# Another written order for the same instructions: block-sparse attention, Fourier mixing and an MLP on one core

## The chip, the core and the metric

The kernel runs on one core of one Trainium2 chip. The core has a matrix engine (TensorE, "PE" in the profile; "PEld" is its weight load), a vector engine (VectorE, "DVE"), a scalar engine (ScalarE, "ACT"), a general engine (GpSimd, "POOL") and an engine that here only issues DMAs (SyncE, "SP"). Each engine works through its own instructions in order; between engines only semaphores order the work. The metric is the device time of one execution in microseconds, the median of several runs.

## The reference

Four batches, eight heads, 768 positions, head size 64. Shortened:

```python
k_rep = k.reshape(B, H, 12, 64, D).mean(axis=3)              # one mean key per block of 64
gate  = einsum('bhsd,bhnd->bhsn', q, k_rep)                  # where(causal by block, gate, -1e9)
sel   = top-3 blocks of gate, and the position's own block
scores = where(sel and causal, q @ k.T / 8, -1e9)
x  = softmax(scores) @ v                                     # heads side by side: (4, 768, 512)
u  = x + real(fft(fft(x, axis=1), axis=2))
un = (u - mean(u)) / sqrt(var(u) + 1e-6)                     # over the last axis
out = u + relu(un @ w_ch1) @ w_ch2                           # 512 -> 2048 -> 512
```

## The kernel before

The work is cut into small steps, each a function that issues a handful of instructions on one or two engines. A step is named by a token with its indices. A long string, `ORDER` (lines 112 to 179), lists 1011 tokens, and one loop at the end of the builder issues them:

```python
with tc.manual_schedule(engines={ET.SP, ET.PE, ET.DVE, ET.Activation, ET.Pool}):
    consts_first()
    for x in ORDER.split():
        n, a = x.split(":")
        WORK[n](*[int(i) for i in a.split(",")])
```

So the order on every engine is the order of the string: no planner moves anything. How tokens of different engines stand to each other in the string has no effect by itself, except where two steps use the same buffer: then the one written first goes first.

**Attention.** The 32 heads are worked in 16 pairs; pair P belongs to batch P // 4. The tokens of a pair, with their engine:

- `Lk`, `Lq`, `Lv` (SP): loads of K, Q and V rows in fp32. Buffers: three for K, three for Q, two for V, so a load waits until the pair before it in the buffer has been used.
- `tk`, `tq` (PE, L292): six transposes into one PSUM tile of 128 × 768. PSUM is a pool of four such buffers, shared by everything that PE produces.
- `ks` (DVE, L297) reduces the transposed K to block sums; `kc` (ACT, L308 or L311) copies the same PSUM tile to fp16. `kh` (DVE) halves the sums. `qc` (DVE, L316) copies Q out of PSUM, `qs` (POOL, L225) casts it.
- `g` (PE) gate products; `gt`, `gx`, `gl`, `gm` (DVE) transpose, take the top three, compare, and transpose back the block mask; `K` (POOL) and `iz`, `Lc`, `Li` put mask and indicator rows where the score product adds them.
- `s:P,i` (PE) scores of query block i; `e` (ACT, L431) the exponential; `d` (POOL, L437) the causal cut on the diagonal; `vc` (POOL) casts V; `v` (PE) product with V; `x` (DVE) division by the row sum.

**Mixing, per batch b.** `fs`, `fd`, `f` (DVE) fold rows into even and odd parts; `pg` (POOL) a guard. `y:b,h` (PE, L519 and L525) is the transform along the sequence. `ty` (ACT, L532) and `tr` (DVE, L538) both copy the tile of `y` out of PSUM, straight and reversed. `m:b,j` (PE, L552 and L553) is the transform along the features; `u` (DVE) adds x and sums, `xu` (ACT) subtracts the mean. `xt` and `un` transpose the result into `unT`: by PE and DVE for batch 0, by two DMA transposes on SP for each `un` of the other batches (L593). `bn`, `nv` (DVE) and `nr` (POOL) find the deviation, which is applied only at the end.

**MLP.** `w:b,i` (PE, L629 and L631) first product, `r` (relu out of PSUM: DVE for every fourth, L639, else ACT, L641), `c:b,j,h` (PE, L656 and L648) second product in two halves, `o:b,j` (DVE, L668) scale and add, `od:b,j` (SP, L673) store of 128 rows, 256 KB (128 KB for the last tile of batch 3, which is split by columns). `W` and `X` (POOL) load the two weight matrices and cast them from fp32 to fp16 on the way, in three and two pieces.

The work of the four batches is interleaved: while PE does the MLP of one batch, the attention of the next pairs and the mixing of the next batch run between its products. Up to the first `w:0` there is only attention and mixing; this text calls it the prologue.

Of the kernel before, what the change touches and what calls it, by code (L numbers as in the profile page):

```python
# [109 lines left out]


ORDER = """
Lk:1 Lq:1 Lk:2 Lq:2 tk:0 ks:0 tq:0 Lq:3 Lk:3 kh:0 qc:0 iz:1 tk:1 qs:0 kc:0 g:0 ks:1 iz:0 gt:0 tq:1
kc:1 gx:0 Lq:4 Lv:0 Lk:4 Lv:1 kh:1 gl:0,0 tk:2 gl:0,1 gm:0 kc:2 qc:1 s:0,3 s:0,2 ks:2 e:0,3 qs:1
tq:2 Lq:5 Lk:5 s:0,5 qc:2 g:1 e:0,5 e:0,2 kh:2 s:0,4 gt:1 qs:2 s:0,0 e:0,4 gx:1 s:0,1 d:0,2 tq:3
gl:1,0 e:0,0 gl:1,1 tk:3 gm:1 e:0,1 d:0,0 qc:3 g:2 d:0,3 kc:3 d:0,5 s:1,5 gt:2 d:0,4 s:1,0 e:1,5
qs:3 ks:3 s:1,4 e:1,0 tq:4 d:0,1 gx:2 vc:0 e:1,4 s:1,3 qc:4 s:1,1 Lv:2 e:1,3 s:1,2 gl:2,0 kh:3
tk:4 gl:2,1 e:1,2 d:1,3 gm:2 g:3 d:1,4 ks:4 d:1,0 v:0 d:1,5 gt:3 vc:1 kc:4 gx:3 e:1,1 s:2,5 Lv:3
Lq:6 LF:0 Lq:7 Lk:6 Lk:7 LT:0 s:2,3 kh:4 gl:3,0 e:2,5 gl:3,1 s:2,4 e:2,3 d:1,1 x:0 tq:5 qs:4 e:2,4
g:4 d:2,3 gm:3 qc:5 s:2,0 d:2,4 s:2,2 d:1,2 e:2,0 gt:4 d:2,5 tk:5 vc:2 gx:4 e:2,2 s:2,1 ks:5 d:2,0  # L120
Lv:4 Lq:8 Lk:8 s:3,1 e:2,1 v:1 gl:4,0 kh:5 gl:4,1 kc:5 d:2,1 gm:4 d:2,2 s:3,2 x:1 e:3,1 vc:3 g:5
e:3,2 Lv:5 Lc:0 d:3,1 s:3,5 gt:5 s:3,0 fs:0,1 e:3,5 s:3,3 d:3,2 gx:5 e:3,0 s:3,4 fs:1,1 tq:6
gl:5,0 e:3,3 fs:0,0 v:2 gl:5,1 fs:1,0 e:3,4 d:3,3 qc:6 d:3,0 s:4,5 x:2 d:3,4 s:4,4 e:4,5 d:3,5
s:4,0 qs:5 v:3 e:4,0 gm:5 fs:2,0 fs:2,1 e:4,4 s:5,5 x:3 s:4,1 e:5,5 s:5,1 e:4,1 fd:2,0 s:4,2 s:5,0
fs:3,1 e:5,1 fs:3,0 s:5,2 fd:2,1 e:5,0 fd:3,1 s:4,3 fd:3,0 e:5,2 tk:6 f:0,1 f:0,2 e:4,3 Lk:9 Lq:9
tk:7 f:0,3 e:4,2 f:0,0 y:0,1 ks:7 pg:0 W:0 kc:6 y:0,0 tr:0,1 d:4,0 kc:7 d:4,4 d:4,5 ks:6 d:5,5
d:4,1 ty:0,1 tr:0,0 s:5,3 d:5,2 s:5,4 d:4,3 kh:6 W:1 ty:0,0 m:0,2 qs:6 e:5,3 u:0,2 m:0,1 vc:4
e:5,4 m:0,0 u:0,1 xu:0,2 d:5,4 tk:8 d:5,1 d:4,2 u:0,0 xu:0,1 d:5,0 xt:0,2 W:2 g:6 un:0,2 xu:0,0
xt:0,1 gt:6 tq:8 un:0,1 kc:8 xt:0,0 qc:8 tq:7 un:0,0 qs:8 v:4 Lq:10 Lk:10 Lv:6 Lq:11 qc:7 bn:0,3
w:0,4 d:5,3 qs:7 bn:0,1 w:0,5 r:0,4 gx:6 ks:8 w:0,6 r:0,5 gl:6,0 kh:7 gl:6,1 x:4 w:0,7 r:0,6 gm:6  # L130
w:0,3 r:0,7 s:6,5 r:0,3 s:6,1 e:6,5 s:6,3 e:6,1 kh:8 s:6,2 fs:4,0 bn:0,4 w:0,2 e:6,2 d:6,1 X:0
e:6,3 g:7 w:0,0 d:6,5 gt:7 r:0,2 d:6,3 vc:6 gx:7 s:6,4 r:0,0 vc:5 s:6,0 e:6,4 tk:9 Li:0 gl:7,0
Lv:7 tq:9 gl:7,1 e:6,0 gm:7 w:0,11 Lq:12 Lv:8 K:7 qc:9 kc:9 g:8 r:0,11 v:5 gt:8 d:6,0 ks:9 w:0,8
qs:9 gx:8 w:0,10 x:5 r:0,8 d:6,4 d:6,2 gl:8,0 s:7,5 s:7,2 r:0,10 kh:9 fs:4,1 w:0,1 bn:0,5 e:7,5
vc:7 e:7,2 tq:10 gl:8,1 Lv:9 r:0,1 X:1 gm:8 s:7,4 qc:10 w:0,15 d:7,2 e:7,4 K:8 bn:0,0 g:9 r:0,15
s:7,0 w:0,9 gt:9 e:7,0 gx:9 vc:8 tq:11 r:0,9 d:7,0 Lv:10 s:7,1 qc:11 d:7,5 tk:10 d:7,4 e:7,1
gl:9,0 s:7,3 ks:10 v:6 e:7,3 kh:10 gl:9,1 kc:10 gm:9 d:7,3 s:8,4 bn:0,2 d:7,1 w:0,12 vc:9 x:6
e:8,4 K:9 Lv:11 Lk:11 Lq:13 Lq:14 Lk:12 Lk:13 v:7 r:0,12 g:10 x:7 s:8,3 w:0,13 e:8,3 gt:10 nv:0
s:9,4 r:0,13 fs:5,1 s:9,1 fs:7,0 vc:11 w:0,14 e:9,4 fs:6,1 e:9,1 fs:7,1 s:8,1 fs:6,0 fs:5,0
c:0,2,0 r:0,14 fd:7,1 fd:6,1 e:8,1 gx:10 s:9,0 fd:7,0 s:9,2 e:9,0 fd:6,0 s:8,2 gl:10,0 c:0,3,0  # L140
f:1,3 e:9,2 f:1,2 e:8,2 gl:10,1 f:1,0 s:8,0 gm:10 s:9,3 d:8,2 e:8,0 y:1,1 d:8,1 d:9,0 e:9,3 nr:0
c:0,0,0 tr:1,1 ty:1,1 s:9,5 c:0,2,1 e:9,5 d:8,0 d:9,3 tk:11 K:10 s:8,5 c:0,1,0 Lk:14 ks:11 kc:11
c:0,3,1 f:1,1 d:9,5 e:8,5 d:9,1 qs:10 tq:12 o:0,2 y:1,0 od:0,2 kh:11 d:8,4 o:0,3 pg:1 vc:10 qc:12
c:0,1,1 od:0,3 ty:1,0 d:9,4 Lv:12 Lv:13 qs:11 tr:1,0 g:11 c:0,0,1 gt:11 d:8,3 d:8,5 gx:11 qs:12
m:1,0 o:0,0 m:1,1 od:0,0 o:0,1 d:9,2 od:0,1 v:8 u:1,1 m:1,2 u:1,0 xu:1,1 c:0,4,0 gl:11,0 xu:1,0
un:1,1 x:8 s:10,3 gl:11,1 un:1,0 c:0,4,1 u:1,2 e:10,3 d:10,3 fs:8,0 s:10,5 s:10,2 bn:1,3 e:10,5
tk:12 e:10,2 fs:8,1 v:9 gm:11 Lk:15 Lq:15 ks:12 xu:1,2 K:11 bn:1,0 tq:13 kc:12 un:1,2 c:0,5,0
qc:13 vc:13 bn:1,4 s:11,2 d:10,5 x:9 s:11,4 vc:12 e:11,2 c:0,5,1 bn:1,1 Lv:14 Lv:15 e:11,4 s:11,0
o:0,5 s:11,5 w:1,11 e:11,5 od:0,5 o:0,4 e:11,0 kh:12 bn:1,5 od:0,4 s:11,3 w:1,7 e:11,3 r:1,11
s:10,1 d:11,3 r:1,7 d:11,0 s:10,0 e:10,1 d:11,4 g:12 d:10,2 tk:13 d:11,5 e:10,0 gt:12 d:11,2  # L150
s:11,1 ks:13 d:10,1 w:1,0 e:11,1 d:10,0 kh:13 fs:9,0 fs:9,1 s:10,4 r:1,0 d:11,1 gx:12 w:1,14
e:10,4 gl:12,0 gl:12,1 g:13 gm:12 r:1,14 d:10,4 w:1,12 K:12 gt:13 kc:13 gx:13 w:1,6 bn:1,2 r:1,12
tq:14 gl:13,0 r:1,6 qs:13 v:10 qc:14 gl:13,1 s:12,3 gm:13 s:12,5 v:11 x:10 e:12,3 K:13 e:12,5
s:12,0 x:11 w:1,8 e:12,0 fs:10,0 vc:15 s:12,1 r:1,8 s:12,2 fs:10,1 s:13,4 e:12,1 d:12,3 w:1,5
fs:11,1 d:12,5 e:13,4 fs:11,0 d:12,1 fd:10,0 w:1,10 r:1,5 fd:11,0 fd:10,1 s:13,0 fd:11,1 r:1,10
w:1,4 f:2,0 e:13,0 f:2,2 s:13,1 f:2,1 e:12,2 w:1,2 e:13,1 tk:14 r:1,4 w:1,3 ks:14 r:1,2 f:2,3
kc:14 s:12,4 kh:14 r:1,3 pg:2 y:2,0 d:13,4 vc:14 nv:1 e:12,4 qs:14 w:1,9 tr:2,0 w:1,13 ty:2,0
# [630 lines left out]
```

## Time and profile before

| | |
|---|---|
| time, median of 3 runs | 297.56 us (297.54 to 297.93) |
| span of the profiled execution | 295.6 us; 1.96 us of the median lie outside it |
| PE busy | 286.5 us (97%) |
| DVE, ACT, POOL busy | 192.5, 164.2, 111.1 us |
| TensorE clock granted | 1.00 throughout |
| DMA | 33.53 MB, mean 113 GB/s |
| row loads, us to landing | K 3.5, Q 3.9 (192 KB), V 4.7 (384 KB) |
| casting loads, us to landing | `W` 8.4 (768 KB), `X` 10.2 (1024 KB) |
| stores, DMA transposes, us to landing | 2.1, 2.5 |
| one copy `kc` of pairs 0 to 6, one reduce `ks` | 0.8, 0.94 us |

In lines of groups and of the timeline the order is: (start,) busy time or duration, engine, line of the kernel, operation, output <- inputs with their shapes, count, and in brackets the idle time before it with what ended it. In the windows each engine's busy time stands beside its number of instructions. In the waits, "A <- B: total, times, longest" is idle time of A that an instruction of B ended.

### The profile page before, as it was taken

How to read it: one execution, taken by the hardware profiler on the slowest of the kernel's cores; microseconds unless marked ns; L12 is line 12 of the kernel's file. 1: busy time of each engine (PE TensorE's matmuls, PEld its weight loads, DVE VectorE, ACT ScalarE, POOL GpSimd, SP SyncE). 2: the span in 40 equal slices, each digit the busy share in tenths (PEclk: the TensorE clock that was granted, in tenths of full speed). 3: DMA queues.
4: the chain of work that ended last, by engine and by line, in shares of the span. 5: the costliest groups of instructions: out<-in, count | busy, mean ns of one | idle time of the engine just before them, and what ended most of it. 6: DMA issues, size and time to landing. Idle time of an engine off the chain costs nothing.

```text
span 295.6 us, 6738 instructions
## 1 busy us (share of the span) xinstructions
PE 286.5 (97%) x2633; PEld 180.2 (61%) x2633; DVE 192.5 (65%) x597; ACT 164.2 (56%) x205; POOL 111.1 (38%) x286
## 2 busy tenths in 40 slices
PE   8899999999999999999999999999999999999995
PEld 4566767765676556656757667446666554555453
DVE  2999999986988638987796577714493282700132
ACT  3698989749578841677788843165524250155000
POOL 2267528528776289064753363220303000110000
PEclk9999999999999999999999999999999999999999
DMA  8999999997999727477000005311000052300023
GB/s 197 268 228 230 262 245 199 195 230 118 226 185 211 168 55 186 118 164 176 3 0 2 0 9 136 38 72 71 2 1 2 32 103 44 142 0 2 0 91 125
DMA packets 93200, 33.53 MB, mean 113 GB/s; under 512 B 85936, under 2 KB 89968, under 8 KB 93168
## 3 DMA queue, kind: packets, MB, share of 16 engines
q1 hardware_dynamic: 87504, 28.47, 40.6%
q0 software_dynamic: 3664, 4.19, 9.1%
q10 hardware_dynamic: 2000, 0.44, 0.7%
q8 instruction: 21, 0.34, 0.5%
q14 instruction: 11, 0.09, 0.1%
HBM read 28.63 MB, written 6.29 MB: 118 GB/s over the span
## 4 chain that ended last, share of the span: by engine, by line
PE 84%; DVE 7%; ACT 6%; DMA 1%; issue 1%; DVEq 0%; ACTq 0%
PE c L656 26%; PE h L629 19%; PE h L631 10%; PE sc L414 7%; PE av L449 6%; ACT pt L431 5%; PE tp L292 5%; PE yp L519 2%; PE mx L552 2%; DVE q L316 2%; PE mx L553 1%; PE warmps L693 1%; DVE u L566 1%; PE g L342 1%; PE c L648 1%; PE sc L409 1%
## 5 line engine op out<-in xcount | busy, mean ns | idle before, releaser
L431 ACT ACTIVATE pt<-sc 128x1024 f16<-128x1024 f32 (+1 forms) x96 | 83.3, 923 | 26.6 <-PE sc L414 19.7
L629 PE MATMUL h<-unT,w 128*128 128x512 f16 x256 | 85.1, 379 | 0.0
L656 PE MATMUL c<-w_sb,hT 128*128 128x512 f16 x368 | 83.8, 379 | 0.0
L631 PE MATMUL h<-unT,w 128*128 128x256 f16 x256 | 69.7, 272 | 0.4 <-DMA unT<-x 0.4
L641 ACT ACTIVATE hT<-h 128x768 f16<-128x768 f32 x48 | 37.8, 813 | 43.7 <-PE h L631 43.7
L656 PEld LDWEIGHTS <-hT 128*128 128x128 f16 x368 | 35.6, 98 | 39.3 <-issue 0.5
L437 POOL TENSOR_SCALAR_AFFINE_SELECT pt<-pt 128x256 f16<-128x256 f16 x96 | 37.5, 414 | 58.5 <-ACT pt L431 57.6
L629 PEld LDWEIGHTS <-w 128*128 128x128 f16 x256 | 25.0, 97 | 29.2 <-issue 1.3
L668 DVE SCALAR_TENSOR_TENSOR u<-c,rs,u 128x512 f32<-128x512 f32 (+1 forms) x25 | 17.5, 725 | 31.2 <-PE c L656 30.4
L639 DVE TENSOR_SCALAR hT<-h 128x768 f16<-128x768 f32 x16 | 15.3, 955 | 29.7 <-PE h L631 29.6
L578 ACT ACTIVATE x<-u,nm 128x512 f16<-128x512 f32 x24 | 15.9, 715 | 22.5 <-DVE nm L572 22.3
L292 PE MATMUL tp<-id,nat 128*128 128x128 f32 x192 | 27.5, 284 | 0.6 <-ACT pt L431 0.3
L631 PEld LDWEIGHTS <-w 128*128 128x128 f16 x256 | 25.0, 98 | 4.3
L225 POOL TENSOR_SCALAR_AFFINE_SELECT qk<-mt 32x160 f16<-32x160 f16 x72 | 23.1, 341 | 10.8 <-DVE mt L386 9.1
L414 PE MATMUL sc<-qk 96*128 96x512 f16 (+3 forms) x144 | 26.8, 305 | 0.0
L225 POOL TENSOR_SCALAR_AFFINE_SELECT qk<-q 64x768 f16<-64x768 f32 (+1 forms) x25 | 20.6, 825 | 14.8 <-DVE q L316 14.1
L292 PEld LDWEIGHTS tp<-id,nat 128*128 128x128 f32 x192 | 22.2, 146 | 5.7 <-issue 1.6
L449 PE MATMUL av<-v,pt 128*128 128x65 f16 x672 | 23.0, 193 | 0.1
L449 PEld LDWEIGHTS <-pt 128*128 128x128 f16 x672 | 22.0, 97 | 1.7 <-POOL pt L437 0.5
L297 DVE TENSOR_REDUCE kr<-tp 128x12 f32<-128x768 f32 x16 | 15.1, 945 | 5.9 <-PE tp L292 5.9
L222 POOL TENSOR_TENSOR t<-vr,rs 128x6 f32<-128x6 f32 x12 | 2.4, 199 | 43.5 <-DVE rs L609 42.9
L414 PEld LDWEIGHTS <-qk 96*128 96x128 f16 x144 | 13.3, 97 | 8.9 <-issue 0.5
(95 smaller groups left out, 351.2 us busy)
## 6 DMA issues: line engine op xcount, KB each, us to landing
nat<-in_v_dram SPq DMA_DIRECT2D x16, 384.0 KB, 4.7
nat<-in_k_dram SPq DMA_DIRECT2D x31, 192.0 KB, 3.5
nat<-in_q_dram SPq DMA_DIRECT2D x31, 192.0 KB, 3.9
out_dram<-u SPq DMA_DIRECT2D x23, 256.0 KB, 2.1
w_sb<-in_moe_w_ch_dram POOLq DMA_DIRECT2D x2, 1024.0 KB, 10.2
w<-in_moe_w_ch_dram POOLq DMA_DIRECT2D x2, 768.0 KB, 8.4
fs_sb<-c_FS SPq DMA_DIRECT2D x1, 582.0 KB, 5.1
w<-in_moe_w_ch_dram POOLq DMA_DIRECT2D x1, 512.0 KB, 7.3
```

The costliest lines, as they stand in the source:

```text
L225: nc.gpsimd.affine_select(out=out, in_=in_, pattern=[[0, i] for i in n], base=0, channel_multiplier=0, compare_op=ALU.is_ge, fill=0.0)
L292: nc.tensor.transpose(ps[:, 128 * st:128 * st + 128], src[:, st, :], id32)
L414: nc.tensor.matmul(ps[:, e, co:co + q1 - q0], qk[0:96, e, 1, 128 * jt:128 * jt + 128], qk[0:96, e, 0, q0:q1], start=True, stop=True)
L431: nc.scalar.activation(out=d["pt"][:, o:o + 2 * n].rearrange("p (e c) -> p e c", e=2), in_=d["sc", i][:, :, 0:n], func=AF.Exp, scale=0.125)
L437: nc.gpsimd.affine_select(out=dg, in_=dg, pattern=[[0, 2], [1, 128]], base=0, channel_multiplier=-1, compare_op=ALU.is_ge, fill=0.0)
L449: nc.tensor.matmul(av[:, e, 66 * st:66 * st + 65], pt[:, co:co + 128], vv[:, e, jt, 0:65], start=(cnt == 0), stop=(cnt == 20))
L578: nc.scalar.activation(out=x_b[:, 2 * kp + k2, :], in_=u_b[:, k2, :], func=AF.Identity, scale=0.0625, bias=nm[:, k2:k2 + 1])
L629: nc.tensor.matmul(hp[:, 0:512], w1s, unT[:, dt, 0:512], start=(dt == 0), stop=(dt == NDT - 1))
L631: nc.tensor.matmul(hp[:, 512:768], w1s, unT[:, dt, 512:768], start=(dt == 0), stop=(dt == NDT - 1))
L641: nc.scalar.activation(out=hT, in_=hp, func=AF.Relu)
L656: nc.tensor.matmul(c_ps[b, g[0]][:, st - g[0], :], h_t[b, it][:, 128 * st:128 * (st + 1)], w2_sb[:, it, :], start=(it == 0), stop=(it == N ...
L668: nc.vector.scalar_tensor_tensor(out=o, in0=ps, scalar=st_t[b][1][:, st:st + 1], in1=o, op0=ALU.mult, op1=ALU.add)
```

## The change

The string is written anew. It holds the same 1011 tokens; only their order differs, on all five engines. It has two lines less, so functions below it stand two lines higher. The diff is one block; here are the lines of it that the text speaks of, in the order of the string.

```diff
-Lk:1 Lq:1 Lk:2 Lq:2 tk:0 ks:0 tq:0 Lq:3 Lk:3 kh:0 qc:0 iz:1 tk:1 qs:0 kc:0 g:0 ks:1 iz:0 gt:0 tq:1
...
-gl:1,0 e:0,0 gl:1,1 tk:3 gm:1 e:0,1 d:0,0 qc:3 g:2 d:0,3 kc:3 d:0,5 s:1,5 gt:2 d:0,4 s:1,0 e:1,5
-qs:3 ks:3 s:1,4 e:1,0 tq:4 d:0,1 gx:2 vc:0 e:1,4 s:1,3 qc:4 s:1,1 Lv:2 e:1,3 s:1,2 gl:2,0 kh:3
...
-tk:7 f:0,3 e:4,2 f:0,0 y:0,1 ks:7 pg:0 W:0 kc:6 y:0,0 tr:0,1 d:4,0 kc:7 d:4,4 d:4,5 ks:6 d:5,5
-d:4,1 ty:0,1 tr:0,0 s:5,3 d:5,2 s:5,4 d:4,3 kh:6 W:1 ty:0,0 m:0,2 qs:6 e:5,3 u:0,2 m:0,1 vc:4
...
-c:0,1,1 od:0,3 ty:1,0 d:9,4 Lv:12 Lv:13 qs:11 tr:1,0 g:11 c:0,0,1 gt:11 d:8,3 d:8,5 gx:11 qs:12
-m:1,0 o:0,0 m:1,1 od:0,0 o:0,1 d:9,2 od:0,1 v:8 u:1,1 m:1,2 u:1,0 xu:1,1 c:0,4,0 gl:11,0 xu:1,0
...
-r:3,12 r:3,9 r:3,14 c:3,0,0 w:3,15 c:3,4,0 r:3,15 c:3,1,0 c:3,0,1 c:3,1,1 c:3,5,0 o:3,0 od:3,0
-o:3,1 c:3,3,0 od:3,1 o:3,5 od:3,5 c:3,4,1 c:3,2,1 o:3,4 od:3,4 c:3,3,1 c:3,5,1 o:3,3 od:3,3 o:3,2
-od:3,2 o:3,6 od:3,6
+Lk:1 Lq:1 Lk:2 Lq:2 tk:0 Lk:3 Lq:3 kc:0 tq:0 ks:0 kh:0 tk:1 qc:0 ks:1 g:0 gt:0 iz:0 iz:1 tq:1 tk:2
+qs:0 Lv:0 Lq:4 Lk:4 Lk:5 Lv:1 Lq:5 Lq:8 Lv:3 Lv:2 Lq:6 Lk:6 Lk:7 LT:0 Lk:8 gx:0 gl:0,0 kh:1 gl:0,1
...
+e:0,1 tq:3 gt:1 tk:3 gx:1 gl:1,0 kh:2 gl:1,1 qs:2 qs:1 d:0,4 qc:3 gm:1 g:2 s:1,5 gt:2 ks:3 s:1,0
+e:0,0 kc:3 s:1,4 tq:4 s:1,3 gx:2 s:1,1 s:1,2 tk:4 e:1,5 qc:4 gl:2,0 gl:2,1 kh:3 d:0,5 d:0,1 qs:3
...
+LF:0 Lv:6 Lk:11 Lq:7 Lq:9 Lv:5 Lk:9 Lk:10 Lv:7 Lq:10 Lq:11 Lq:14 Lv:9 kh:5 s:3,1 x:1 kc:5 e:2,1
...
+f:0,2 f:0,3 f:0,0 f:0,1 e:5,0 tk:7 kc:7 y:0,1 ks:7 y:0,0 tr:0,1 tk:6 tr:0,0 e:5,2 ty:0,1 kc:6 s:5,3
+ks:6 ty:0,0 e:5,3 m:0,2 s:5,4 kh:7 kh:6 u:0,2 e:5,4 m:0,1 u:0,1 m:0,0 g:6 u:0,0 xu:0,2 d:4,2 d:4,1
+d:4,0 d:5,5 d:5,0 W:1 qs:6 d:4,3 d:4,4 W:0 vc:6 vc:4 d:4,5 d:5,4 d:5,3 pg:0 d:5,1 d:5,2 vc:5 W:2
...
+d:9,4 qs:11 d:9,5 K:10 tq:12 c:0,2,1 g:11 o:0,0 e:9,0 kc:11 v:8 f:1,2 qc:12 f:1,0 y:1,0 gt:11 gx:11
+gl:11,0 y:1,1 o:0,2 tr:1,0 gl:11,1 gm:11 ty:1,0 c:0,1,0 ty:1,1 tr:1,1 x:8 s:10,0 m:1,1 tk:12 u:1,1
+ks:12 c:0,1,1 o:0,1 kc:12 pg:1 vc:12 K:11 d:9,0 s:11,5 m:1,0 v:9 m:1,2 u:1,0 u:1,2 e:10,0 e:11,5
...
+gt:15 e:13,3 f:2,2 y:2,0 ty:2,0 y:2,1 tr:2,0 s:13,0 ty:2,1 s:13,5 c:1,1,1 v:12 o:1,1 c:1,4,0 o:1,0
+m:2,0 e:13,0 c:1,5,0 tr:2,1 gx:15 m:2,1 e:13,5 c:1,2,0 gl:15,0 u:2,0 m:2,2 gl:15,1 u:2,1 u:2,2 gm:15
+c:1,3,0 xu:2,0 xu:2,2 xu:2,1 od:0,4 od:1,0 od:1,1 od:0,0 Lv:13 un:2,2 un:2,1 un:2,0 K:14 d:13,3
...
+r:2,15 f:3,3 y:3,1 r:2,9 ty:3,1 tr:3,1 f:3,1 c:2,1,1 o:2,1 y:3,0 ty:3,0 c:2,0,1 m:3,0 tr:3,0 o:2,0
+m:3,1 c:2,4,0 c:2,5,0 m:3,2 c:2,2,1 c:2,3,1 c:2,4,1 u:3,0 c:2,5,1 u:3,1 bn:3,2 bn:3,3 u:3,2 xu:3,0
...
+c:3,4,1 c:3,1,1 c:3,2,0 o:3,4 c:3,2,1 c:3,0,1 c:3,3,0 o:3,1 c:3,3,1 o:3,2 o:3,0 c:3,5,1 o:3,3 od:2,5
+od:3,5 od:2,2 od:2,3 od:3,2 od:3,4 od:3,1 od:2,4 od:3,0 od:3,3 o:3,6 od:3,6
```

## The prediction

> **What bounds the kernel now.** I read the page's first and fourth parts, then the windows, the waits, and the timeline of three places.
>
> ```profile
> span 295.6 us, 6738 instructions
> PE 286.5 (97%) x2633; PEld 180.2 (61%) x2633; DVE 192.5 (65%) x597; ACT 164.2 (56%) x205; POOL 111.1 (38%) x286
> ...
> PE 84%; DVE 7%; ACT 6%; DMA 1%; issue 1%; DVEq 0%; ACTq 0%
> ```
>
> TensorE carries the end, with 9 us idle in all. The change keeps every instruction, so its work stays; only gaps can grow or shrink. The windows place them (second figure: length, third: PE busy).
>
> ```profile
> 0.00:12.00 12.00, 9.70 (x51) 5.92 (x52) 6.41 (x29) 5.37 (x7) 2.50 (x18) 1.00 1.00 224
> 12.00:24.00 12.00, 11.29 (x162) 7.51 (x162) 11.56 (x39) 10.01 (x14) 7.19 (x15) 1.00 1.05 238
> 24.00:36.00 12.00, 11.48 (x216) 8.12 (x213) 11.23 (x54) 11.35 (x15) 7.12 (x14) 1.00 1.05 242
> 36.00:48.00 12.00, 10.92 (x198) 9.08 (x195) 11.38 (x27) 11.22 (x16) 4.87 (x12) 1.00 1.01 241
> 48.00:58.60 10.60, 9.91 (x134) 7.61 (x134) 10.19 (x26) 9.23 (x12) 6.97 (x14) 1.00 1.14 193
> 58.60:100.00 41.40, 41.40 (x423) 26.34 (x420) 35.12 (x137) 29.34 (x36) 24.14 (x53) 1.00 1.02 199
> 100.00:150.00 50.00, 49.62 (x473) 32.07 (x472) 36.30 (x114) 30.04 (x38) 31.43 (x81) 1.00 0.47 109
> ```
>
> Before 58.6 us, where the first `w` (first MLP product, batch 0) starts, PE idles 5.3 us over five windows; from there to 150 only 0.4, and from 150 to 250 nothing. Issue spacing tells more than busy time: against the shortest spacing of each kind of token, 11.6 us are lost before 58.6 and 2.7 us after it. In the prologue ACT and DVE set the pace, not PE: of the 36 us from 12 to 48, DVE is busy 34.2 and ACT 32.6. ACT runs from its first exponential at 12.6 to the end of `xu:0,0` at 55.9 with 2.8 us idle; `w` follows 2.7 us later. The clock (third figure from the end) is 1.00 in all rows.
>
> Three places matter. First, ACT and DVE around pair 3's K:
>
> ```profile
> 18.09 0.84 ACT L308 CAST qk<-tp 128x768 f16<-128x768 f32 x1
> 18.77 4.40 ACT L431 ACTIVATE pt<-sc 128x256 f16<-128x256 f32 x5
> 23.99 0.80 ACT L308 CAST qk<-tp 128x768 f16<-128x768 f32 x1 [0.82 <-DVE kr L297]
> ```
> ```profile
> 19.61 0.94 DVE L297 TENSOR_REDUCE kr<-tp 128x12 f32<-128x768 f32 x1
> ```
>
> `kc:3` (copy) runs at 18.09, `ks:3` (reduce of the same PSUM tile) after it at 19.61. For pair 4 the order is the reverse, and ACT stands 0.82 us until the reduce ends. So the two readers of one tile go one after the other, in the written order. The same holds for `ty` and `tr`, which read one `y` tile:
>
> ```profile
> 112.46 1.03 ACT L532 CAST ty<-yp 128x772 f16<-128x772 f32 x1 [2.68 <-PE yp L519]
> 113.52 1.02 DVE L538 CAST tr<-yp 128x768 f16<-128x768 f32 x1 [0.38 <-ACT ty L532]
> 116.23 0.27 PE L552 MATMUL mx<-fd_sb,ty 128*128 128x256 f16 x1
> ```
>
> `y:1,0` ends at 112.4, both copies at 114.5, and `m` starts at 116.2: 1.7 us of slack. Third, the end, where `o` and its store alternate:
>
> ```profile
> 282.65 10.37 SPq L673 DMA_DIRECT2D out_dram<-u  x7
> ...
> 290.42 1.41 DVE L668 SCALAR_TENSOR_TENSOR u<-c,rs,u 128x512 f32<-128x512 f32 x2 [2.70 <-PE c L656]
> 292.17 0.48 DVE L668 SCALAR_TENSOR_TENSOR u<-c,rs,u 128x256 f32<-128x256 f32 x1 [0.34 <-PE c L648]
> ```
>
> The last store is issued at 292.68 and lands at 294.41. Stores that follow at once are issued 0.66 us apart (282.65 and 283.31; 192.93 and 193.59).
>
> **The change, part by part.** Nothing is added or removed. The sum is made on the profiled execution: span 295.6, which is 1.96 us under the median of 297.56; I keep that difference.
>
> *Casting loads* (POOL). They are issued in the order 1, 0, 2; X:0 and X:1 stay before their use. In the profile W lands after 8.4 us and X after 10.2. From the POOL work ahead of them I place W:2 at about 58 and its first use at about 75, X:0 at about 80 with use at 96, X:1 at 86 with use at 106. Cost 0, under 16 to 20 us of PE work each; with the cover gone, up to one landing, 10 us.
>
> *Row loads* (SP). Many go earlier, and several are queued behind a load that waits for a buffer: Lq:7 and Lq:9 behind Lk:11 (waits tk:7), Lv:9 behind Lq:14 (waits tq:9). Q and K loads land in 3.5 to 3.9 us, V in 4.7; their transposes come 6 us or more after the release. Cost 0. PE hardly waits for a load before either, so nothing is won. The stores od:0,0 to od:0,4 go far later; `u` of the next batch reuses their buffers, but comes 2 us or more after they land: 0.
>
> *Prologue* (ACT, DVE). The same 51 ACT tokens precede the end of `xu:0,0`, so ACT's added idle moves `w`.
> - `kc:0` is now ahead of `ks:0`: 0.80 us of copy before DVE's chain, which starts near 7.3 instead of 6.68: +0.6, of which 0.3 stays, as ACT then waits elsewhere.
> - `ks:3` is now ahead of `kc:3`, in a DVE queue that is full to that point, so it ends near 20.6 as now (19.61 + 0.94). `kc:3` waits for it, and `e:1,5` and the rest are queued behind: about 2.3 us of ACT idle. Of that, 0.5 returns where the 0.82 us at `kc:4` shrinks: +1.8.
> - `ks:7` waits for `kc:7`, which is now behind `e:5,0` on ACT; `tr:0,1` is queued behind `ks:7`, and `ty:0,1` is now behind `tr:0,1` (same tile): one copy, +1.0.
>
> Together +3.1, bounds +1.0 (the last alone) to +4.5.
>
> *Middle* (PE behind `w` and `c`). Every wait here is PE time.
> - Batch 1: the order is y:1,0, y:1,1, with `tr:1,0` ahead of `ty:1,0` but `ty:1,1` ahead of `tr:1,1`: four copies in a row, 1.02 + 1.03 + 1.03 + 1.02 = 4.1 us. `m:1,1` needs the PSUM buffer that the fourth frees, and PE has only y:1,1 and c:0,1,0 in between (1.02 + 1.72): 1.3. `m:1,0` waits for `o:0,1` (0.75 us) right after c:0,1,1, with 0.1 us of `s` between: 0.9. `tk:12` waits for `x:8`, and `y:1,1` for `o:0,2`: 0.45.
> - Batch 2: `s:13,5` waits for ty:2,0, then tr:2,0 (2.05 us and two hand-overs) behind y:2,1 and one `s` (1.45): 0.7. The six DMA transposes of `un:2`, 1.3 us apart and 2.5 us to landing, begin 3 us after `m:2,2`; the last lands after 3 + 6.5 + 2.5 = 12, while PE has 11.7: 0.6 (0.3 to 1.3, as some take 3.7 or more).
> - Batch 3: `f:3,1` is queued behind `tr:3,1`: 1.04 + 1.02 + 0.7 after y:3,1, against 2.0 us of PE work: 0.8. `un:3` has four `c` tokens (6.9 us) after `m:3,2` to hide under, where it had five: 0.3 (0 to 1).
> - `un:1` 0.2, and five short ties in which PE follows a just finished `x`, `kh`, `K` or `d`: 0.8.
>
> That is 6.1 us of waits in place of the 2.7 there now: +3.4, bounds +1.0 (some ties already cost that in the present 2.7) to +6.
>
> *End* (SP). od:3,2 now stands ahead of od:3,4, 3,1, 2,4, 3,0, 3,3 and 3,6. It waits for `o:3,2`, hence for c:3,3,1, the last product but one. It can go at 291.20, as the first store after that product does now; three stores that could have gone before (od:3,4, 3,1, 2,4) are behind it. od:3,6 is the seventh: 291.20 + 6 × 0.66 = 295.16, where it is issued at 292.68 now: +2.5. Below, 1.9, if the issue spacing shrinks to 0.56 in a long run; above, 4.4, if seven stores share what the best slice of the page moved (268 GB/s, 1.64 MB in 6.1 us after 291.2, and 1.5 us to landing).
>
> The rows of the stores are thus 0.66 us from issue to issue against 2.1 us from issue to landing. The Trainium skill, page "DMA: Bandwidth & Descriptors", section "Issuing engines are not separate DMA queues", holds that starting DMAs on several engines saves only the sequencer's time to initiate them, which is usually small relative to the DMA itself. By that sentence a place further back in SP's queue would cost next to nothing, the end would grow only by the 0.3 us by which `o:3,6` comes later behind three other `o`, and the whole sum would be 304.4 us.
>
> Sum: 3.1 + 3.4 + 2.5 = +9.0. 297.56 + 9.0 = **306.6 us** (span about 304.6).
>
> **Rivals.**
> 1. *Faster: ACT's gaps close.* Place: ACT between 12.6 and 55.9. The row loads come earlier and `kc` and `e` are regrouped; if `tk:3` and `ks:3` get far enough ahead of ACT that the tile is reduced by 18.1, ACT never waits. Price: its 2.8 us of idle, and at most the 5.3 us of PE idle there. It decides the total only if the tail's stores also overlap; the time is then 297.6 − 2.8 = 294.8. Against it: DVE has no gap before 19.6 in which to do the reduce.
> 2. *Only the end shows.* The prologue finds other work for ACT, and the middle's ties are covered as now: 297.6 + 2.5 = 300.1. For it: 2.7 us of ties now, after a similar number of tight places. Against it: each of the places in batch 1 is one sum of copies against less PE work.
> 3. *All upper bounds add:* 4.5 + 6 + 4.4 = 14.9, or 312.5. For it: a late `w` shifts ACT's load into a busier stretch. Against it: waits in a row often share one cause.
> 4. *Nothing moves,* since PE's order matters little: 297.6. The end speaks against it.
>
> **How the numbers follow.** The forecast case (302.5 to 309.5) gets 0.61, rival 2 (298.2 to 302.5) 0.15, rival 3 (above 309.5) 0.14, rival 1 0.07, rival 4 0.03. A measurement of this kernel tells 0.2% (0.6 us) from no change. Faster is rival 1: 0.07; same is rival 4: 0.03; slower the rest: 0.90. The range leaves out rivals 1 and 4, and about 0.1 shared between the far ends of 2 and 3: 300.0 to 311.5.
>
> **What would show it.** Right: a wait of ACT's copy at L306 (`kc`, two lines up from 308) for DVE's reduce of over 2 us near 18 to 21; the first `w` at 61 to 62; `tr` and `ty` waits above 1 us in batch 1; waits of PE at `mx` for DVE; seven stores in one row after the last-but-one product, the last issued 2.5 us or more after the last `o`. Wrong: a first `w` at or before 58.6, PE as full between 100 and 250 as now, or a last store within 0.5 us of its `o`. A wait of PE for `w` or `w_sb` by DMA would mean that a casting load is not covered.

## The result and the profile after

The changed order takes 314.84 us (314.25 to 315.86), the order before 297.61 us beside it: 1.058 times as long, interval 1.056 to 1.060. 306.6 us were predicted, at most 311.5. The profiled execution has a span of 312.9 us, 17.3 more than before.

The page, first and fourth part:

```profile
span 312.9 us, 6733 instructions
PE 289.0 (92%) x2633; PEld 180.8 (58%) x2633; DVE 198.7 (63%) x597; ACT 165.1 (53%) x205; POOL 115.7 (37%) x286
...
PE 66%; DVE 23%; ACT 3%; POOL 2%; issue 2%; SPq 1%; DMA 1%; DVEq 0%; ACTq 0%; POOLq 0%
```

PE's busy time grew by 2.5 us, and its share of the chain fell from 84% to 66%: most of the time is in waits. The lines numbered in this profile stand two lower than before. The windows:

```profile
12.00:24.00 12.00, 9.34 (x136) 6.18 (x132) 10.57 (x39) 8.84 (x12) 5.67 (x11) 1.00 1.09 245
48.00:58.60 10.60, 7.12 (x62) 5.06 (x60) 8.36 (x14) 6.25 (x8) 6.36 (x10) 0.84 1.09 198
100.00:150.00 50.00, 47.63 (x374) 28.79 (x372) 31.88 (x92) 28.55 (x36) 22.54 (x57) 1.00 0.50 117
```

From 12 to 24 PE lost 2 us more than before, from 48 to 58.6 it is busy for 7.1 us of 10.6, and the granted clock there is 0.84 where it was 1.00. From 100 to 150 it idles 2.4 us instead of 0.4.

To place all of it, I sum over PE's tokens the time from one token's start to the next beyond the shortest such time of its kind in the profile before ("PE waits" from here on; what a lowered clock adds counts as well). The first `w` starts at 65.9 us instead of 58.6, although `tq:7` comes ahead of it no longer.

| part | before | after | added | predicted |
|---|---|---|---|---|
| prologue, to the first `w` | 11.6 | 19.5 | 8.0 | 3.1 |
| middle, from there to the last product | 2.7 | 9.1 | 6.3 | 3.4 |
| end, from the last product's end to the span's | 3.5 | 6.5 | 3.1 | 2.5 |

These sum to 17.4, against 17.3 us of span. All three parts went the way that was forecast; the prologue is where most of the difference lies. The largest single wait there, on DVE, POOL and PE:

```profile
49.51 3.74 DVE L496 COPY mid<-zw 128x6 f16<-128x6 f16 x1
51.86 1.38 DVE L295 TENSOR_REDUCE kr<-tp 128x12 f32<-128x768 f32 x1
```
```profile
49.04 0.95 POOL L721 DMA_DIRECT2D w<-in_moe_w_ch_dram  x1
50.02 0.83 POOL L223 TENSOR_SCALAR_AFFINE_SELECT qk<-q 128x768 f16<-128x768 f32 x1
50.80 0.76 POOL L435 TENSOR_SCALAR_AFFINE_SELECT pt<-pt 128x256 f16<-128x256 f16 x2
51.51 0.76 POOL L721 DMA_DIRECT2D w<-in_moe_w_ch_dram  x1
52.29 1.76 POOL L223 TENSOR_SCALAR_AFFINE_SELECT v<-nat 128x768 f16<-128x768 f32 x2
```
```profile
53.30 0.43 PE L523 MATMUL yp<-fs_sb,mid 128*128 128x193 f16 x3 [3.35 <-DVE kr L295]
```

`f:0,1` ends with a copy of six columns into `mid`. A copy of this shape takes 0.17 us in the order before with POOL idle, 0.38 us here beside a cut, and 3.74 us at this place, beside the first casting load, W:1, and the POOL row behind it. PE, in the middle of `y:0,0`, needs `mid` and waits 3.35 us. The bracket names the reduce, but the matmul reads `mid` (its operand says so), and both DVE records end within 0.01 us of each other: a releaser that the profile infers is to be checked against the operands. Then TensorE's clock (third figure from the end) drops:

```profile
50.00:51.00 1.00, 0.00 (x0) 0.00 (x0) 1.00 (x1) 0.64 (x1) 0.98 (x2) 1.00 1.17 266
...
54.00:55.00 1.00, 1.00 (x9) 0.99 (x7) 0.42 (x1) 0.79 (x1) 0.40 (x2) 0.56 1.10 197
55.00:56.00 1.00, 1.00 (x6) 0.55 (x6) 0.59 (x1) 0.14 (x1) 0.00 (x0) 0.50 1.17 205
```

Behind the prologue the waits stand where the prediction put most of them: `m:1,0` for `o:0,1`, `s:13,5` for `tr:2,0`, `w:2,2` for `un:2`.

```profile
130.95 0.27 PE L550 MATMUL mx<-fd_sb,ty 128*128 128x256 f16 x1 [0.73 <-DVE u L666]
...
188.40 0.27 PE L412 MATMUL sc<-qk 96*128 96x128 f16 x2 [0.71 <-DVE tr L536]
...
212.15 0.38 PE L627 MATMUL h<-unT,w 128*128 128x512 f16 x1 [0.87 <-DMA unT<-x]
```

And the end, where seven stores go in one row while the last product ends at 306.4:

```profile
304.71 2.46 DVE L666 SCALAR_TENSOR_TENSOR u<-c,rs,u 128x512 f32<-128x512 f32 x4 [2.70 <-PE c L654]
305.49 3.77 SPq L671 DMA_DIRECT2D out_dram<-u  x7
```

### The profile page after: what moved, and what is told of

It reads as the page before. It is cut to its first block, busy times and chain, and to the rows that moved or that the text cites. A ratio compares the mean times of both kernels' runs of the same rounds, so it can differ in the third digit from the quotient of the medians.

```text
span 312.9 us, 6733 instructions
## 1 busy us (share of the span) xinstructions
PE 289.0 (92%) x2633; PEld 180.8 (58%) x2633; DVE 198.7 (63%) x597; ACT 165.1 (53%) x205; POOL 115.7 (37%) x286
## 4 chain that ended last, share of the span: by engine, by line
PE 66%; DVE 23%; ACT 3%; POOL 2%; issue 2%; SPq 1%; DMA 1%; DVEq 0%; ACTq 0%; POOLq 0%
PE c L654 22%; PE h L627 15%; PE h L629 8%; PE sc L412 5%; PE av L447 4%; PE tp L290 4%; DVE q L314 2%; DVE kr L295 2%; DVE mx L364 2%; DVE u L666 2%; DVE x L220 2%; PE mx L550 1%; PE mx L551 1%; PE warmps L691 1%; ACT ty L530 1%
## 5 line engine op out<-in xcount | busy, mean ns | idle before, releaser
L435 POOL TENSOR_SCALAR_AFFINE_SELECT pt<-pt 128x256 f16<-128x256 f16 x96 | 40.4, 446 | 70.1 <-ACT pt L429 58.9
L666 DVE SCALAR_TENSOR_TENSOR u<-c,rs,u 128x512 f32<-128x512 f32 (+1 forms) x25 | 17.4, 722 | 32.9 <-PE c L654 29.5
L223 POOL TENSOR_SCALAR_AFFINE_SELECT qk<-mt 32x160 f16<-32x160 f16 x72 | 24.1, 355 | 14.0 <-DVE mt L384 6.6
L576 ACT ACTIVATE x<-u,nm 128x512 f16<-128x512 f32 x24 | 15.9, 713 | 17.2 <-DVE nm L570 16.9
L309 ACT CAST qk<-tp 64x768 f16<-64x768 f32 x18 | 14.3, 793 | 10.6 <-DVE kr L295 9.1
```

The source lines that it names most:

```text
L223: nc.gpsimd.affine_select(out=out, in_=in_, pattern=[[0, i] for i in n], base=0, channel_multiplier=0, compare_op=ALU.is_ge, fill=0.0)
L435: nc.gpsimd.affine_select(out=dg, in_=dg, pattern=[[0, 2], [1, 128]], base=0, channel_multiplier=-1, compare_op=ALU.is_ge, fill=0.0)
L666: nc.vector.scalar_tensor_tensor(out=o, in0=ps, scalar=st_t[b][1][:, st:st + 1], in1=o, op0=ALU.mult, op1=ALU.add)
```

## Experiments: the casting load in the prologue

The gains from here on are against the 314.84 us of the changed order. The order before, run beside each group of experiments, stood at 297.5 to 298.2 us, so a gain of 0.7 us or less is not told from none.

Two ways to take the casting load away from the copy, by POOL's order alone. First, both loads ahead of the cuts:

```diff
-... d:4,2 d:4,1 d:4,0 d:5,5 d:5,0 W:1 qs:6 d:4,3 d:4,4 W:0 vc:6 ...
+... W:1 W:0 d:4,2 d:4,1 d:4,0 d:5,5 d:5,0 qs:6 d:4,3 d:4,4 vc:6 ...
```

> The changed order with only W:1 and W:0 moved, on POOL, from among the cuts and casts of pairs 4 to 6 to ahead of d:4,2. Theory (the casting loads are issued on POOL beside a DVE copy, f:0,1 copying one column group into mid, which then takes 3.74 us instead of 0.17; y:0,0 waits for it, and PE, idle for 3.4 us, is then granted half its clock for 3.6 us): the copy takes under 0.6 us, PE's wait inside y:0,0 goes, no slice at half clock, and the time falls by 4 to 5 us, to about 310.3 us. Rival (the chain kc:7, ks:7, tr:0,1, ty:0,1 sets the prologue's end anyway, the long copy only hides it): the time falls by 1 us at most.

Measured: 311.69 us, 3.15 us faster. The copy takes 0.80 us and ends as `qs:6` ends; no window between 40 and 62 us is below a clock of 1.00; PE's wait in `y:0,0` is 0.6 us. The gain lies between theory and rival: of the 5 us or so that wait and clock had cost PE, a part comes back as waits at `s:5,3`, `m:0,2`, `xt` and `tk:8`.

Second, the token that stood ahead of the first casting load in the order before:

```diff
-... d:5,0 W:1 qs:6 ... d:5,3 pg:0 d:5,1 ...
+... d:5,0 pg:0 W:1 qs:6 ... d:5,3 d:5,1 ...
```

> The changed order with only pg:0 moved, on POOL, to directly ahead of W:1, as pg:0 stands ahead of the first casting load in the order before. pg:0 reads what the four f of batch 0 write, so POOL then starts no casting load before f:0,1 is done. Theory (a casting load issued during DVE's copy to mid holds that copy up for 3.7 us): the copy takes under 1 us and the time falls by as much as with W:1 and W:0 moved ahead, 3.1 us, to about 311.7 us; the cuts behind it come some 0.3 us later. Rival (it is POOL's uninterrupted row of operations, not the casting load, that holds the copy): the copy stays over 2 us and the time at 314.8 us.

Measured: 311.43 us, 3.4 us faster.

```profile
49.86 0.17 DVE L496 COPY mid<-zw 128x6 f16<-128x6 f16 x1
```
```profile
50.00 0.18 POOL L505 COPY gone<-fg 1x4 f16<-1x4 f16 x1 [0.56 <-DVE fg L220]
50.13 0.96 POOL L721 DMA_DIRECT2D w<-in_moe_w_ch_dram  x1
```

POOL now stands until the folding is done, then starts the load 1.1 us later than in the changed order, and the copy is as short as anywhere. So the place of one guard token, whose result nothing uses, was worth 3.4 us. In the order before, `pg:0` kept load and copies apart in just this way; the last copy of the folding there ends at 45.45:

```profile
45.28 0.17 DVE L494 COPY fg<-zw 128x6 f16<-128x6 f16 x1
```
```profile
45.42 0.18 POOL L507 COPY gone<-fg 1x4 f16<-1x4 f16 x1 [6.82 <-DVE fg L222]
45.55 0.95 POOL L723 DMA_DIRECT2D w<-in_moe_w_ch_dram  x1
```

What holds the copy? Trials on idle engines, added behind the last store of the order before:

```diff
+    def port(k):
+        nc.gpsimd.tensor_copy(out=gone, in_=mid[0:1, 0, 0:4])
+        nc.vector.tensor_copy(out=lt[0:1, 0, 0:4], in_=gone)
+        if k in (1, 3, 4, 5):
+            load_w1({1: 1, 3: 2, 4: 0, 5: 1}[k])
+        if k in (2, 3, 5):
+            ... five cuts of 128 x 256 in place ...
+        for _ in range(16):
+            ... copy (or addition, 4 and 5) of 128 x 6 into mid ...
```

> The order before, with six short trials added behind the last store, when no other engine works; their results are not used. In each, DVE runs 16 times the copy of 128 x 6 that f:0,1 makes (trials 0 to 3) or an addition of the same shape (4 and 5), beside POOL: trial 0 nothing, 1 a casting load (768 KB), 2 five cuts as d makes them, 3 a casting load and then five cuts, 4 a casting load (512 KB), 5 a casting load and five cuts. Theory (a casting load keeps DVE's copies out until it has been worked off): one copy of over 2 us in trials 1 and 3, copies of 0.2 to 0.8 us in trial 2, additions hardly touched in 4. Rival (only the row of POOL's operations behind the load keeps them out): trial 1 shows no copy over 1.2 us, trial 3 one of over 2 us.

Measured, in one execution: both fell. The timeline of trials 1 and 3, the copies in groups of 16:

```profile
296.80 3.65 DVE L750 COPY mid<-qk 128x6 f16<-128x6 f16 x16
297.03 0.83 POOL L723 DMA_DIRECT2D w<-in_moe_w_ch_dram  x1 [0.34 <-issue]
...
305.25 4.33 DVE L750 COPY mid<-qk 128x6 f16<-128x6 f16 x16
305.46 0.76 POOL L723 DMA_DIRECT2D w<-in_moe_w_ch_dram  x1 [0.32 <-issue]
306.23 2.44 POOL L744 TENSOR_SCALAR_AFFINE_SELECT qk<-qk 128x256 f16<-128x256 f16 x5
```

Sixteen copies beside a load take 3.65 us, 3.41 us without one: the longest single copy is 0.42 us in trial 1 and 0.53 us in trial 3, and it ends when the load's issue ends. Cuts let the copies in between them. So a casting load by itself holds a copy only for the rest of its 0.76 to 0.95 us of issue.

Three further orders of POOL around W:1 tell apart what else it takes.

```diff
-... qs:2 qs:1 d:0,4 ...                                            (W:2 behind vc:5)
+... qs:2 qs:1 W:2 d:0,4 ...
```

> The changed order with only W:2 moved, on POOL, to ahead of d:0,4 near 14 us, so that W:1 near 49 us is no longer the first casting load of the program. Theory (the first casting load of a program holds DVE's copy for 4.2 us from its issue): the copy to mid takes under 1.2 us, 2.5 to 3.5 us faster. Rival (the row of POOL operations W:1, qs, d, d, W:0, vc, all without a gap, keeps the port): 3.7 us as before, the time within 1 us of 314.8, less what W:2 takes from the row loads.

Measured: the copy takes 1.19 us and ends with `qs:6`; 313.9 us, 0.9 us faster, which is not clear of noise (ratios 1.049 to 1.057 here, 1.056 to 1.060 for the changed order). PE's wait in `y:0,0` falls from 3.6 to 1.0 us, but behind `s:1,4`, at 19 us, PE now waits 2.7 us instead of 1.5, and from 21.9 to 25.3 us its clock stands at 0.50, which takes most of it back.

```diff
-... W:1 qs:6 d:4,3 d:4,4 W:0 vc:6 vc:4 d:4,5 ...
+... W:1 qs:6 d:4,3 d:4,4 vc:6 vc:4 W:0 d:4,5 ...
```

> The changed order with only W:0 moved, on POOL, from behind d:4,4 to behind vc:4. Theory (first casting load): the copy ends 4.2 us after the issue of W:1 as before, 3.7 us long. Rival (POOL's row; the copy gets in at the end of vc:6): vc:6 ends 0.76 us earlier, and the copy is 3.0 us long. Second rival (the second load, W:0, is what prolongs it): under 2.2 us.

Measured: 314.89 us, no change, and a copy of 3.81 us. It ends 4.28 us after the start of W:1, with `vc:4`; in the changed order it ended 4.21 us after it, with `vc:6`. W:0 plays no part.

```diff
-... W:1 qs:6 d:4,3 d:4,4 W:0 ...
+... W:1 d:4,3 d:4,4 qs:6 W:0 ...
```

> The changed order with only qs:6 moved, on POOL, from directly behind W:1 to behind d:4,4, so that two cuts of 0.4 us follow the load instead of the cast of fp32 rows. Theory (first casting load): the copy ends 4.2 us after the issue of W:1. Rival (the cast right behind the load takes the port that the copy waits for; cuts let it in, as the added trials showed): the copy takes under 1.2 us, and the time falls by 2.5 us or more.

Measured: 311.29 us, 3.5 us faster. The copy, here from the three profiles in turn (W:2 early, W:0 late, qs:6 late):

```profile
51.06 1.19 DVE L496 COPY mid<-zw 128x6 f16<-128x6 f16 x1
```
```profile
49.00 3.81 DVE L496 COPY mid<-zw 128x6 f16<-128x6 f16 x1
```
```profile
49.70 0.47 DVE L496 COPY mid<-zw 128x6 f16<-128x6 f16 x1
```

In these three, as in the changed order, the copy starts 0.47 us after the load's issue. With two cuts of 0.4 us behind the load, it gets in as that issue ends. In these runs it takes both things for the long hold: the load is the program's first, and a cast of fp32 rows stands right behind it (3.74 to 3.81 us, in all six profiles with this order). With cuts in place of the cast the copy waits for the rest of the issue, 0.47 us; with another load long before it waits for the issue and the cast, 1.19 us, although the cast began after the copy did:

```profile
50.59 0.77 POOL L721 DMA_DIRECT2D w<-in_moe_w_ch_dram  x1
51.37 0.84 POOL L223 TENSOR_SCALAR_AFFINE_SELECT qk<-q 128x768 f16<-128x768 f32 x1
```

Each of these two cases was seen in one profile. Why the first load prolongs the hold to 4.2 us was not settled; no run here shows what POOL does then beyond its rows.

## Experiments: the two readers of one tile, and the rest of the prologue

```diff
-... gt:2 ks:3 s:1,0 e:0,0 kc:3 s:1,4 ...
+... gt:2 s:1,0 e:0,0 kc:3 ks:3 s:1,4 ...
```

> The changed order with only kc:3 ahead of ks:3, so that ACT's copy need not wait for DVE's reduce of the same tile. Theory (ACT sets the pace of the prologue; its 2.0 us of idle before kc:3 is paid in full or nearly): the first w comes 1.3 to 2 us earlier, 313.2 us. Rival (the wait only moves to DVE, whose reduce and then gates come later, and to the later stops of the prologue): under 0.5 us.

Measured: 313.36 us, 1.5 us faster; first `w` at 64.3 us. In the changed order and then here:

```profile
20.88 0.80 ACT L306 CAST qk<-tp 128x768 f16<-128x768 f32 x1 [2.02 <-DVE kr L295]
```
```profile
18.01 0.84 ACT L306 CAST qk<-tp 128x768 f16<-128x768 f32 x1
```

ACT's 2.0 us of idle go. How much of it reaches the end is known only roughly: the ratios lie at 1.050 to 1.056 here and 1.056 to 1.060 in the changed order. And in this profile the first score, `s:0,3`, which the edit does not touch, already starts at 11.05 us instead of 11.75; over the profiles with this start unedited it lies between 10.81 and 11.82. So of the 1.6 us by which the first `w` comes earlier, 0.9 can be put down to the swap.

Five moves of the prologue together, among them `ks:7` ahead of `kc:7`, as in the order before:

```diff
+W:1 W:0 ahead of d:4,2; kc:3 ahead of ks:3; ks:0 ahead of kc:0
+ks:7 ahead of kc:7; ty:0,1 ahead of tr:0,1
```

> The changed order with five moves in the prologue: W:1 and W:0 ahead of d:4,2; kc:3 ahead of ks:3; ks:0 ahead of kc:0; ks:7 ahead of kc:7; ty:0,1 ahead of tr:0,1. Theory (these carry the prologue's 8 us of added PE waits: 3.1 and 1.5 measured for the first two, 0.8 for the DVE start, 1.0 for the four copies at y:0): first w near 59.5 us, time 308.4 us. Rival (something else in the prologue, such as the place of kc, e and the gates among each other, paces it once these are gone): first w over 62 us, time over 310 us.

Measured: 313.37 us, only 1.5 us faster, less than the first move alone. A move of mine made a new wait: `kc:7` on ACT now waits 3.1 us for `ks:7`, which is queued on DVE behind the folding, and the exponentials of pair 5 are queued behind `kc:7`. PE then waits 1.4 us at `tk:6`, and the clock falls to 0.5 again.

```profile
48.73 1.60 ACT L309 CAST qk<-tp 64x768 f16<-64x768 f32 x2 [3.06 <-DVE kr L295]
```
```profile
50.39 0.87 PE L290 MATMUL tp<-id,nat 128*128 128x128 f32 x6 [1.38 <-ACT qk L309]
```

In the order before, the folding was done earlier relative to ACT's row; the same pair of tokens has another price in another row. Without the last two moves, and with `pg:0` for W:

```diff
+pg:0 ahead of W:1; kc:3 ahead of ks:3; ks:0 ahead of kc:0
```

> The changed order with three moves in the prologue: pg:0 ahead of W:1, kc:3 ahead of ks:3, ks:0 ahead of kc:0. Theory (three causes that add: 3.4, 1.5 and 0.8 us): 309.1 us, the first w near 60.4 us. Rival (the copies at y:0 pace the end of the prologue whatever comes before): 310.5 us or more.

Measured: 309.34 us, 5.5 us faster, first `w` at 60.7 us. The guard alone gave 3.4 us, so `kc:3` and `ks:0` together gave 2.1; 0.6 for `ks:0` is what is left beside 1.5, and was not measured by itself. PE waits in the prologue are 14.3 us against 11.6 before. Of these last 2.7 us this profile shows 1.1 at the copies of `y:0`, the prediction's third term, where the order before has 0.3: `ty` on ACT waits for `tr:0,1`, and PE twice for `ty`.

```profile
49.85 1.04 ACT L530 CAST ty<-yp 128x772 f16<-128x772 f32 x1 [0.91 <-DVE tr L536]
```
```profile
50.94 0.27 PE L550 MATMUL mx<-fd_sb,tr 128*128 128x256 f16 x1 [0.56 <-ACT ty L530]
52.53 0.39 PE L407 MATMUL sc<-qk 64*128 64x512 f16 x2 [0.56 <-ACT ty L530]
```

No run took these waits away by themselves; the rest was not traced further.

The row loads by themselves, in the order before:

```diff
-... tq:0 Lq:3 Lk:3 ... Lq:4 Lv:0 Lk:4 Lv:1 ... Lq:5 Lk:5 ... Lv:2 ... Lv:3 Lq:6 LF:0 Lq:7 Lk:6 Lk:7 ...
+... Lk:3 Lq:3 Lv:0 Lq:4 Lk:4 Lk:5 Lv:1 Lq:5 Lq:8 Lv:3 Lv:2 Lq:6 Lk:6 Lk:7 LT:0 Lk:8 ...    (SP alone)
```

> The order before, with only SP's row loads of the first 30 us in the changed order: the 21 from the start to Lk:8 (Lv:0 to Lv:3, Lk:4 to Lk:8, Lq:4 to Lq:8 and the transform's table go earlier). Theory of the prediction (row loads are covered in both orders): within 0.6 us of 297.5. Rival (loads in the changed order keep PE from its transposes, part of the prologue's late g and s): 1 us slower or more, with new waits of PE for a load.

Measured: 298.15 us beside 298.21, ratio 0.9999 (0.998 to 1.002). In this part of the program the row loads are covered in both orders. The later loads were not tried by themselves.

## Experiments: the middle and the end

```diff
-... y:1,1 o:0,2 tr:1,0 gl:11,1 gm:11 ty:1,0 c:0,1,0 ty:1,1 tr:1,1 ...
+... y:1,1 o:0,2 gl:11,1 gm:11 ty:1,0 tr:1,0 c:0,1,0 ty:1,1 tr:1,1 ...
```

> The changed order with only ty:1,0 ahead of tr:1,0, so that three copies instead of four lie between y:1,0 and the PSUM buffer that s:10,0 and m:1,1 wait for. Theory: the 0.98 us that PE loses at s:10,0 and m:1,1 go, 313.9 us. Rival (the next wait, s:11,5 and m:1,0 for o:0,1, takes them up): under 0.3 us.

Measured: 314.21 us, 0.6 us faster, between the two; the intervals of this run and of the changed order overlap. In the profile the wait at `s:10,0` and `m:1,1` (0.98 us) is gone and the one behind it stays at 0.9: the middle's PE waits fall from 9.07 to 8.31 us.

Six places at once:

```diff
+ty:1,0 ahead of tr:1,0; o:0,2 ahead of gt:11; kh:12 ahead of ks:13
+s:13,5 behind c:1,1,1; un:2,0 ahead of un:2,2; f:3,1 ahead of tr:3,1
```

> The changed order with six moves behind the prologue: ty:1,0 ahead of tr:1,0; f:3,1 ahead of tr:3,1; s:13,5 behind c:1,1,1; un:2,0 ahead of un:2,2; kh:12 ahead of ks:13; o:0,2 ahead of gt:11. Theory (each of these waits of PE was paid in full: 0.98, 0.56, 0.87, 1.03, 0.83, 0.51 us): the time falls by 4 to 4.7 us, to 310.4 us. Rival (what PE saves at one place it waits at the next, since ACT, DVE and POOL are loaded there too): under 2.5 us.

Measured: 310.33 us, 4.5 us faster. The middle's waits fall by 4.1 us, from 9.1 to 5.0, and the profiled span by 4.2. Behind the prologue PE is the bound, and its waits are paid one to one.

```diff
-... o:3,2 o:3,0 c:3,5,1 o:3,3 od:2,5 od:3,5 od:2,2 od:2,3 od:3,2 od:3,4 od:3,1 od:2,4 od:3,0 od:3,3 ...
+... each of these od directly behind its o ...
```

> The changed order with only the last ten stores of SP moved: each directly behind its o. Theory (od:3,2 holds up six stores behind it; they are issued 0.5 us apart and then share the DMA engines): the end falls by 3.0 us, to 311.8 us, with the last store issued about 0.5 us after the last product's end instead of 2.2 us. Rival (the stores' bytes set the end, wherever they are issued): under 1 us.

Measured: 313.16 us, 1.7 us faster. The end shrinks from 6.5 to 4.9 us, not to 3.5: `o:3,0` still comes behind `o:3,2`, so beside `od:3,6` three stores are left after the last product but one, where the order before has two. The same edit the other way round, in the order before:

```diff
-... c:3,3,1 c:3,5,1 o:3,3 od:3,3 o:3,2 od:3,2 o:3,6 od:3,6
+... c:3,3,1 o:3,2 c:3,5,1 o:3,3 o:3,6 ... od:3,2 od:3,4 od:3,1 od:2,4 od:3,0 od:3,3 od:3,6
```

> The order before, with o:3,2 directly behind c:3,3,1 and the eleven last stores in the changed order, od:3,2 ahead of six others. Theory (this alone is what the end costs): 3.0 us slower, 300.6 us. Rival (the end in the changed order is late for another reason, such as o:3,0 behind o:3,2): under 1.5 us slower.

Measured: 300.39 us beside 297.47, ratio 1.0095 (1.008 to 1.011), 2.9 us slower, with `o:3,2` one product earlier as the only other move. The seven stores stand in one row as in the changed order:

```profile
291.12 3.77 SPq L673 DMA_DIRECT2D out_dram<-u  x7
```

All moves together, first with the five of the prologue:

> The changed order with the five moves of the prologue, the six behind it, every last store directly behind its o, and o:3,0 ahead of c:3,3,1. Theory (three separate causes that add): 6.4 from the prologue, 4.5 from the middle, 2.6 from the end, 301.3 us, so 4 us over the order before stay unexplained. Rival (the causes cover one another): over 305 us.

Measured: 307.19 us, 7.7 us faster, where the theory had 301.3; the prologue keeps the new wait at `kc:7`. With the three moves that held, the six of the middle, the stores behind their `o` and `o:3,0` ahead of c:3,3,1:

> The same three moves, with the six moves behind the prologue and the stores at the end as in the run with all moves. Theory (prologue, middle and end add): 309.1 - 4.5 - 2.3 = 302.3 us. Rival (something is shared): over 304 us.

Measured: 302.75 us, 12.1 us faster, near the theory's 302.3: the three parts add. Against the order before (ratio 1.017, 1.015 to 1.019) 5.3 us are left, in PE waits 2.5 in the prologue, 2.1 in the middle and 0.8 at the end. No order tried here beats the order before.

## Why the prediction was wrong in its size

The direction, the three places and most of the mechanisms held. The sum of 9.0 missed 17.2 by four terms.

- **Casting loads, "Cost 0".** This step failed, and is the largest: 3.4 us (the guard moved back), 3.1 us (loads moved ahead). It asked only when W lands and when it is used, which was right: no PE wait for W appears. It did not ask what stands beside its issue: the first load held a DVE copy for 3.74 us, PE waited 3.35 us for that copy, and then ran 3.4 us at half clock. The diff showed `pg:0` going from ahead of the first W to far behind, and `pg` was named in the description as a guard, but it was given no price. The cover was a wait.
- **Prologue, `kc:3` and `kc:0`.** 1.8 and 0.3 predicted; 2.1 measured for both together, 1.5 (roughly) for `kc:3` alone. **`ks:7` and `tr:0,1`**, 1.0 predicted: once the hold of the copy is gone, the profile shows PE waiting 1.1 us for `ty` there, against 0.3 at that place in the order before. The one run that turned both pairs round got slower where it should have gained, by the wait at `kc:7`, so the price of this term was not measured. About 1.9 us more of the prologue stayed unexplained.
- **Middle, +3.4.** The list of waits was near: 6.1 us forecast, 6.7 us for the eight places seen (1.0 at `s:10,0` and `m:1,1`, 0.9 at `m:1,0`, 0.5 at `y:1,1`, 0.9 at `s:13,5`, 1.0 at `w:2,2`, 0.6 in `y:3,0`, and 0.8 at `g:12` and 1.0 near `s:9,3`, which were among the ties given 0.8 together). What failed is the subtraction of the 2.7 us of before. Only 0.54 of it was one large wait; the rest is spread over the other tokens in amounts under 0.4 us, and 2.4 us of that kind are in the changed order too. New waits add to it and do not replace it. `un:3` and `un:1`, 0.5 together, did not show.
- **End, +2.5.** 3.1 in the profile, 2.9 in the order before. The issue part was over-estimated: the last store is issued 2.2 us after the last product's end, 0.55 before, hence 1.7 us, as the spacing is 0.37 to 0.68 us and not 0.66. In its place the landing grew by 0.9: 2.7 us for the last 128 KB, where it took 1.7; and 0.4 us more lie between that landing and the span's end. The upper bound had this sharing in it, with 1.5 us to landing, a figure that no row shows.

What the prediction worked out from the Trainium skill, page "DMA: Bandwidth & Descriptors", section "Issuing engines are not separate DMA queues", that a place further back in SP's queue costs next to nothing, did not come: the order of the stores cost 2.9 us. The page's sentence speaks of starting DMAs on several engines, which no run here tried; it does not tell what a store waits behind another in one queue.

Of the rivals, "all upper bounds add", 312.5 us, came nearest, with the right parts and for the wrong reason: its 4.5 us for the prologue were exceeded by a mechanism that no bound held. "Faster" fell at its deciding point, as `kc:3` started at 20.9 and not by 18.1. "Only the end shows" fell with the middle's waits. The range was too narrow at the top, since a term given as 0 carried no upper bound into it, although the text named 10 us as its price with the cover gone.

## What to carry to other kernels

When an order changes, list the waits that a moved token used to impose on the work behind it: a token that does nothing but wait may be what keeps two operations apart, and its cover belongs into the range with its price. Where an engine is the bound, add the new waits to the small losses that are there; do not net one against the other. A pair of tokens has no price by itself: the swap that gained time at pair 3 made a wait of 3.1 us at pair 7, because the row ahead of it on the other engine was longer.

## What the runs showed of the hardware

- A DVE copy of 128 x 6 in fp16, 0.17 us alone, waited for the POOL operation in progress: 0.80 us beside a cast of fp32 rows, 0.42 to 0.53 us beside the issue of a casting load. So the text's opening sentence, that between engines only semaphores order the work, is too narrow here: the held copy's record waits for no semaphore. The Trainium skill, page "SBUF — State Buffer", section "Who interferes with whom", says that a DVE copy in one of its two-port modes and a GpSimd instruction exclude each other for the whole instruction, and that issue order decides who blocks. These rows agree, though none shows in which mode the copy ran. The 1.19 us do not agree, since the cast that went ahead of the waiting copy began after it; and where cuts followed the load instead, the copy went first. The 3.74 to 3.81 us behind a program's first casting load with a cast right behind it go further: in the changed order a cast, two cuts, a second load and another cast began and ended while the copy stood.
- Around the gap of 3.35 us without a matmul TensorE was granted 0.50 of its clock, for 3.4 us in the changed order and for 6.8 us in two other profiles with the same hold of the copy (each store behind its `o`; `ty:1,0` ahead of `tr:1,0`). The lowered clock comes in steps of 3.41 us, and where the step falls makes the difference. In the changed order, and then with the stores behind their `o`, PE's busy time is the first figure behind the length:

```profile
50.70:54.11 3.41, 0.81 (x10) 0.82 (x11) 3.02 (x3) 0.35 (x1) 3.40 (x7) 1.00 1.12 188
54.11:57.53 3.42, 3.42 (x27) 2.57 (x25) 1.86 (x2) 2.36 (x4) 0.29 (x1) 0.50 1.17 199
```
```profile
48.26:51.67 3.41, 1.63 (x16) 1.01 (x13) 3.41 (x6) 2.41 (x3) 3.38 (x7) 1.00 1.07 231
51.67:55.08 3.41, 1.71 (x11) 1.60 (x12) 2.12 (x3) 1.03 (x1) 2.79 (x4) 0.50 1.04 167
```

  In the ten places, over all profiles, where the clock halved with matmuls still to come, PE had been busy for 0.10 to 0.51 of the step before; it did not halve behind steps of 0.52 and more, nor behind one of 0.49. In the run with `ks:7` ahead of `kc:7` that step (0.39 busy) held several shorter waits, the longest 1.4 us. With the wait in `y:0,0` gone the clock stayed at 1.00 there. The Trainium skill, page "TensorE: Matmul & The Clock Gate", section "Part 1: The HAM clock gate (the "warmup" mystery)", gives one idle window of about 3.4 us as the point at which the clock halves; the length of the steps agrees, but here a step that was half busy was enough.
- Seven stores issued in one row went out 0.37 to 0.68 us apart, and the last landed 2.7 us after its issue.
